# The last 1024 tokens of a bilinear feed-forward as a two by two block product with seven products

## The chip, the cores and the metric

The kernel runs on one core of one Trainium2 chip. Its engines are TensorE (PE, matrix products), VectorE (DVE), ScalarE (ACT), GpSimd (POOL) and SyncE (SP, which issues most of the transfers). Each engine works through its own list of instructions in order, and waits on semaphores for the others. The metric is device time in microseconds (us). Three runs of the kernel before took 397.61, 400.4 and 403.2 us, median 400.4.

## The reference

A forgetting attention over 8 batches, 8 heads, 576 positions, 64 features per head, then a bilinear feed-forward over its 4608 tokens of 512 features. Cut to what matters:

```python
cum = np.cumsum(np.log(np.clip(f, 0.0001, 1.0)), axis=-1)
scores = q @ k.T / 8 + cum[:, :, :, None] - cum[:, :, None, :]   # masked above the diagonal
attn = softmax(scores) @ v
x = attn.transpose(0, 2, 1, 3).reshape(4608, 512)
a = x @ w_a            # w_a, w_b: 512 x 1536
b = x @ w_b
out = (a * b) @ w_out  # w_out: 1536 x 512
```

## The kernel before

The kernel builds a list of small operations (`Op`), each with an engine (or several that may do it), the operations it depends on, and a function that issues its instructions. Two written-out lists decide the rest: `ORDER` (L1212 on) gives the numbers of the operations in the order in which they are issued, and with it the order on every engine; `CHOICE` (L1324 on) gives the engine of each operation that can run on more than one, in order of their numbers. `SLOTS` (L141 on) gives the buffer of a ring that each new tile takes. Nothing is planned at run time.

**Attention.** An attention step t (0 to 31) is a pair of heads of one batch (four steps per batch). Its scores are matmuls (qk, into PSUM tiles "sc"), DVE adds the decay and takes the maximum (max, L674, into "S"), ACT takes the exponential (exp, L701 and L705, into PA and PB), DVE the reciprocal (L715), POOL divides (norm, L726), SP transposes PA and PB through the DMA engines into PTA and PTB (tr, L740), PE multiplies with v (pv, into "pvx"), and ACT or DVE copies the result into xT (ev). xT is four tiles of 128 features by 4608 tokens, f16; it is both the result of the attention and the left input of the feed-forward.

**Feed-forward.** The tokens are cut into chunks of 256, 256, 256, 384, six times 512, and 384 (L1206). For each chunk and each of the 12 column blocks of 128 of the 1536, `ff_mm` (L1056) makes a (PSUM tile "psa") and b ("psb"): four blocks of 128 features, each as two matmuls of 64 output rows (`mm_halves`, L72), so eight matmuls for a group. ACT copies psa to f16 (acopy, L1064, tile "a16"), DVE multiplies psb with it (mul, L1070) into a tile "ht". `ff_out` (L1078) multiplies ht with w_out for 128 tokens at a time, in three parts of four column blocks, eight matmuls each (pso); ACT or DVE copies the result (ocopy) and SP stores it. The last 128 tokens are stored in three pieces ("psz", L1093 on). psa, psb, pso and psz share a ring of four PSUM banks ("ff"); the ring "sc" has two PSUM tiles of two banks.

The feed-forward of early chunks is woven into the attention of later batches: its matmuls fill PE while the other engines work on the softmax. A chunk can start when all its tokens have been copied into xT. In the order before, pv30 and pv31, the last two attention products, stand ahead of the last output group of a 512-token chunk, and behind them come a 512-token and a 384-token chunk with nothing beside them.

Numbers: the operations of the feed-forward begin at 1707. A column block (two, for the 256-token chunks) has four numbers (psa, acopy, psb, mul), a block of 128 tokens five (three pso, ocopy, store).

Of the kernel before, what the change touches and what calls it, by code (L numbers as in the profile page):

```python
# [25 lines left out]
def kernel(  # L26
# [19 lines left out]
    NP = H // 2  # L46
# [25 lines left out]
    def mm_halves(out, lhsT, rhs, **kw):  # L72
        for r in HP:
            nc.tensor.matmul(out=out[r], lhsT=lhsT[:, r], rhs=rhs, **kw)  # L74
# [30 lines left out]
    def paddings():  # L105
# [36 lines left out]
        PA:03210213021302130213021302130213;PB:01101010101010101010101010101010;S:010110100110100110101011001101  # L142
        01010101001010101010101010010011010100101001000100010011011010011100111011010101110101;a16:0210210210210
        21021021021021021021201201210210210210201201201012012021021021020120120201010201210201201201201201021;bc
        :0210210210210210210210210210;ff:03120312032100023120310323231232301230103010103203013120312031203120312
        03123012310120213203203013203210312013201320130123021312312031232013012013023103210131310321320312031023
        10210321032130230231023102312302130213021321023023012032032031310210210312310231302132013203210310231023
        20120210102120321312012013203103021301321301302102302310230132031203120132013012012021023101301321032132
        030231031031032031230123201230312312312312312312302311021021302301231231230;ht:0dcba981234567d0bc9a18234
        5670dbc9a182543d670cb9a1428653d70cb2a9154863d7bac025914863dcb7a9205148dc36a9b72051483cdb6;n16:0110100101  # L150
        10001010010101010101;n32:0210201201201201020101212110210220201212202101;nv:01010101;osb:0101010101001010
        10101010010100110101;qd:010101010101010101010101;sc:0101010101010101010101011010010101100010101011001001
        0101101010101011010101010101010100101011101100101010110101100101100100101010;st:054321503421503421503421
        50342150
# [922 lines left out]

    def ff_out(t0, tb, part):  # L1078
        if part == 0:
            T[("pso", t0, tb)] = ff_tile([128, 512], FP32, "pso")  # L1080
        o = T[("pso", t0, tb)]
        for fb in range(4 * part, 4 * part + 4):
            mm_halves(o, T[("ht", t0, fb)][:, 128 * tb:128 * tb + 128], wout16[:, fb, :],
                      start=(fb == 0), stop=(fb == 11))
# [8 lines left out]
    def last_out(t0, tb, part, x):  # L1093
        lo, hi = PIECES[x]
        if part == 0:
            T[("psz", x)] = ff_tile([128, 512], FP32, "psz")
        o = T[("psz", x)]
        for fb in range(4 * part, 4 * part + 4):
            mm_halves(o[:, 0:hi - lo], T[("ht", t0, fb)][:, 128 * tb:128 * tb + 128], wout16[:, fb, lo:hi],
                      start=(fb == 0), stop=(fb == 11))  # L1100
# [19 lines left out]
    def chain(o, which):  # L1120
        o.deps.extend(last_ff[which][-1:])
        last_ff[which].append(o)

    def ffn(t0, n):
# [29 lines left out]
        for tb in range(n // 128):  # L1154
            p = base + 12 + tb
            if t0 + 128 * tb + 128 == NT:
                for x, (e, d) in enumerate((("ACT", 0.39), ("ACT", 0.25), ("DVE", 0.25))):
                    prev = []
                    for part in range(3):
                        mo = Op("PE", 4 * (PIECES[x][1] - PIECES[x][0]) * COLS * 1.012,  # L1160
                                lambda _, tb=tb, part=part, x=x: last_out(t0, tb, part, x),
                                list(dict.fromkeys(m for m, _ in muls[4 * part:4 * part + 4])) + prev + w_ops[("o", part)],
                                prio=5000 + p + 0.1 * part + x, mode="full", name="psz")
                        chain(mo, "out")
                        if part == 0:
                            uo = take(mo, "ff")
                        else:
                            uo.append(mo)
                        for _, hu in muls[4 * part:4 * part + 4]:
                            hu.append(mo)  # L1170
                        prev = [mo]
                    oc = Op(e, d, lambda e, x=x: last_copy(e, x), prev, prio=-2000 + p, name=f"ocopy{x}")
                    uo.append(oc)
                    ou = take(oc, "osb" if x == 2 else "S")
                    so = Op("ACT" if x == 1 else "SP", 0.53, lambda _, tb=tb, x=x: last_store(t0, tb, x), [oc],
                            prio=-500 + p, land=packets(128, 1024))
                    ou.append(so)
                continue
            prev = []
            for part in range(3):  # L1180
                mo = Op("PE", 4 * 512 * COLS * 1.012, lambda _, tb=tb, part=part: ff_out(t0, tb, part),
                        list(dict.fromkeys(m for m, _ in muls[4 * part:4 * part + 4])) + prev
                        + w_ops[("o", part)],
                        prio=5000 + p + 0.1 * part, mode="full", name="pso")
                chain(mo, "out")
                if part == 0:
                    uo = take(mo, "ff")
                else:
                    uo.append(mo)
                for _, hu in muls[4 * part:4 * part + 4]:  # L1190
                    hu.append(mo)
                prev = [mo]
            oc = Op(None, {"ACT": 0.59, "DVE": 0.69}, lambda e, tb=tb: ff_ocopy(e, t0, tb), prev, prio=-2000 + p, name="ocopy")
            uo.append(oc)
            ou = take(oc, "osb")
            so = Op("SP", 0.53, lambda _, tb=tb: ff_store(t0, tb), [oc], prio=-500 + p, land=packets(128, 2048))
            ou.append(so)

# [7 lines left out]
    cuts = [256, 256, 256, 384] + [512] * 6 + [384]  # L1206
    assert sum(cuts) == NT
    t0 = 0
    for n in cuts:
        ffn(t0, n)  # L1210
        t0 += n
    ORDER = """  # L1212
        0 1 29 30 46 2 52 62 5 3 31 37 32 38 33-36 39 40 42 41 53 47 58 4 43 267 262 279 6-9 54 48 10 56
# [160 lines left out]
```

## Time and profile before

| what | value |
|---|---|
| three runs | 397.61, 400.4, 403.2 us; median 400.4 |
| profiled execution, span | 397.5 us |
| PE busy | 386.4 us, 97% |
| DVE, ACT, POOL busy | 293.0, 290.6, 257.8 us |
| psa, psb matmuls | 1056 each, 114.1 and 113.9 us busy |
| pso matmuls | 840, 102.4 us busy |
| acopy of 512 columns | 90, mean 581 ns |
| mul of 512 columns | 90, mean 686 ns |
| chain that ended last, shares | PE 77%, DMA 11%, POOL 4%, ACT 3% |

A row of the groups reads: line, engine, operation, output<-input with shapes, count | busy us, mean ns of one | idle time of the engine ahead of them and what ended it. A row of the timeline reads: start us, duration us, engine, line, operation, output<-input, count of instructions run together, and in square brackets the idle time before. Matmuls are pipelined, so the duration of a row is longer than the distance between two starts; the distance is what a matmul costs PE. The profile's own time for the execution is its span; the fastest of the three runs lies 0.1 us above it.

### The profile page before, as it was taken

The numbers are of one execution on the slowest core, as the hardware profiler recorded it, in microseconds if no ns is written. First come the engines' busy times: TensorE is split into PE (matmuls) and PEld (weight loads), VectorE is DVE, ScalarE is ACT, GpSimd is POOL, SyncE is SP. The second block draws the span as 40 slices with busy tenths as digits, with TensorE's granted clock in tenths as the row PEclk, the third lists the DMA queues.
The fourth block names the chain that finished last, engine by engine and source line by source line (L and its number), as shares of the span: only waits on it lengthen the run. The fifth ranks groups of instructions, "written<-read, shape, count | busy, mean of one in ns | idle before, by whom it ended". The sixth has DMA issues, their size and how long they took to land.

```text
span 397.5 us, 14691 instructions
## 1 busy us (share of the span) xinstructions
PE 386.4 (97%) x5768; PEld 250.9 (63%) x5768; DVE 293.0 (74%) x971; ACT 290.6 (73%) x805; POOL 257.8 (65%) x464
## 2 busy tenths in 40 slices
PE   6899999999999999999999999999999999999997
PEld 3557887969766665655555665555555556567785
DVE  7888798999998779787888798668878772333131
ACT  5999899999879778778988588898878763232131
POOL 8689687769887679884996877779936871000000
PEclk9999999999999999999999999999999999999999
DMA  7999999999999999999999999999999586100202
GB/s 117 256 195 167 157 147 226 220 285 283 244 188 228 238 293 234 235 249 292 231 205 278 223 255 214 248 258 206 252 220 230 104 147 156 63 2 1 81 28 81
DMA packets 147365, 76.87 MB, mean 193 GB/s; under 512 B 124384, under 2 KB 128352, under 8 KB 147296
## 3 DMA queue, kind: packets, MB, share of 16 engines
q1 hardware_dynamic: 132856, 68.72, 77.7%
q0 software_dynamic: 14256, 7.08, 14.7%
q8 instruction: 45, 0.74, 0.8%
q14 instruction: 24, 0.20, 0.2%
q10 hardware_dynamic: 184, 0.14, 0.1%
HBM read 52.05 MB, written 9.58 MB: 155 GB/s over the span
## 4 chain that ended last, share of the span: by engine, by line
PE 77%; DMA 11%; POOL 4%; ACT 3%; issue 2%; DVE 2%; SPq 0%; DVEq 0%; ACTq 0%; POOLq 0%
PE psa L74 21%; PE psb L74 20%; PE pso L74 20%; PE sc L551 4%; DMA PTA<-PA 3%; PE pvx L769 3%; POOL PA L726 2%; DMA PTB<-PB 2%; PE psT L359 2%; DMA wb<-in_moe_w_b_dram 2%; PE sc L539 2%; DMA wout<-in_q_dram 2%; PE sc L74 1%; PE psP L74 1%; DMA k<-in_k_dram 1%
## 5 line engine op out<-in xcount | busy, mean ns | idle before, releaser
L674 DVE CUSTOM_DVE_ANT_0 S<-sc,spread 64x576 f32<-64x576 f32 (+4 forms) x232 | 125.9, 562 | 17.3 <-ACT PA L705 8.3
L74 PE MATMUL psb<-xT,wb 128*64 128x512 f16 (+2 forms) x1056 | 113.9, 341 | 0.8 <-DMA wb<-in_moe_w_b_dram 0.5
L74 PE MATMUL psa<-xT,wa 128*64 128x512 f16 (+2 forms) x1056 | 114.1, 341 | 0.0
L289 ACT CAST a<-psa 128x512 f16<-128x512 f32 (+1 forms) x114 | 63.3, 559 | 56.4 <-PE psa L74 52.3
L1073 DVE TENSOR_TENSOR ht<-psb,a 128x512 f16<-128x512 f32 (+1 forms) x114 | 74.4, 658 | 38.5 <-PE psb L74 27.7
L74 PE MATMUL pso<-wout,ht 128*64 128x512 f16 x840 | 102.4, 380 | 0.0
L726 POOL TENSOR_SCALAR PA<-PA,st 128x256 f16<-128x256 f16 (+2 forms) x180 | 84.9, 483 | 8.8 <-DVE st L715 5.5
L705 ACT ACTIVATE PA<-S,st 128x256 f16<-128x256 f32 (+2 forms) x168 | 84.2, 504 | 6.5 <-DVE st L674 6.0
L74 PEld LDWEIGHTS <-wb 128*64 128x64 f16 x1056 | 62.5, 110 | 30.0 <-issue 2.5
L74 PEld LDWEIGHTS <-wa 128*64 128x64 f16 x1056 | 61.7, 110 | 29.3 <-issue 2.2
L726 POOL TENSOR_SCALAR PB<-PB,st 128x512 f16<-128x512 f16 (+1 forms) x90 | 63.4, 711 | 24.3 <-DVE st L715 10.7
L74 PEld LDWEIGHTS <-ht 128*64 128x64 f16 x912 | 49.9, 110 | 33.0 <-issue 1.9
L705 ACT ACTIVATE PB<-S,st 128x512 f16<-128x512 f32 x56 | 40.2, 720 | 3.3 <-DVE st L674 3.0
L705 ACT ACTIVATION_READ_ACCUMULATOR PA<-S,st 128x1 f32 x168 | 32.1, 191 | 0.0
L701 ACT ACTIVATE PB<-S,st 128x576 f16<-128x576 f32 x28 | 21.7, 775 | 9.8 <-POOL PA L726 3.1
L631 POOL TENSOR_SCALAR_AFFINE_SELECT spread<-spread 128x768 f32<-128x768 f32 x24 | 20.9, 870 | 10.1 <-DMA spread<-cum_d 10.0
L769 PEld LDWEIGHTS <-nv 128*64 128x64 f16 x640 | 21.7, 110 | 7.5 <-DMA PTA<-PA 2.1
L674 DVE CUSTOM_DVE_ANT_1 S<-sc,spread 128x256 f32<-128x256 f32 x48 | 19.8, 419 | 6.9 <-PE sc L539 2.0
L715 DVE RECIPROCAL st<-st 128x2 f32<-128x2 f32 x128 | 18.3, 156 | 6.9 <-ACT PB L705 3.5
L674 DVE DVE_READ_ACCUMULATOR2_ANT st<- 128x1 f32 (+1 forms) x280 | 23.0, 82 | 0.0
L551 PE MATMUL sc<-kT,qT 64*128 64x512 f16 (+4 forms) x144 | 20.8, 326 | 1.2 <-ACT kT L289 0.4
L289 ACT COPY osb<-pso 128x512 f32<-128x512 f32 x24 | 13.8, 580 | 9.1 <-PE pso L74 7.8
(106 smaller groups left out, 483.2 us busy)
## 6 DMA issues: line engine op xcount, KB each, us to landing
spread<-cum_d SPq DMA_DIRECT2D x24, 576.0 KB, 6.4
out_dram<-osb SPq DMA_DIRECT2D x35, 256.0 KB, 3.4
q<-in_q_dram SPq DMA_DIRECT2D x14, 576.0 KB, 5.7
k<-in_k_dram SPq DMA_DIRECT2D x14, 576.0 KB, 5.0
v<-in_v_dram SPq DMA_DIRECT2D x24, 256.0 KB, 6.0
wout<-in_moe_w_out_dram POOLq DMA_DIRECT2D x3, 512.0 KB, 7.5
nv<-in_v_dram POOLq DMA_DIRECT2D x8, 128.0 KB, 5.1
wa<-in_moe_w_a_dram POOLq DMA_DIRECT2D x2, 512.0 KB, 7.5
```

Of the source, the lines that this page charges most:

```text
L74: nc.tensor.matmul(out=out[r], lhsT=lhsT[:, r], rhs=rhs, **kw)
L289: nc.scalar.copy(out=out_, in_=in_)
L359: nc.tensor.matmul(out=p[m][HP[j] if quad else slice(0, 128), 64 * t:64 * t + 64], lhsT=x[r, j, t, :] if quad else x[r, t, :], rhs=ident16 ...
L551: nc.tensor.matmul(out=dst, lhsT=lhsT, rhs=rhs, start=start, stop=stop, skip_group_check=True)
L631: nc.gpsimd.affine_select(out=c[:, :, 0:SM].rearrange("p h (j k) -> p h j k", k=128), in_=c[:, :, SM:2 * SM].rearrange("p h (j k) -> p h j ...
L674: nc.vector.tensor_tensor_reduce(out=o, in0=x, in1=y, scale=-1.0, scalar=3e38, op0=ADD, op1=MIN, accum_out=m)
L701: nc.scalar.activation(out=p_blocks(t, 4), in_=T[("s" if direct else "z", t, 4)], func=EXP, bias=st[:, 8:9], scale=sign, accum_out=st[:, 1 ...
L705: nc.scalar.activation(out=p_blocks(t, i)[:, :, h, :], in_=(T[("s", t, i)][:, h, :] if direct else T[("z", t, i)][:, h * n:h * n + n]).rea ...
L715: nc.vector.reciprocal(out=st[:, 20 + 2 * i:22 + 2 * i], in_=st[:, 10 + 2 * i:12 + 2 * i])
L726: VEC[e].tensor_scalar(out=p, in0=p, scalar1=st[:, c:c + 1], scalar2=1.0, op0=MUL, op1=MUL)
L769: nc.tensor.matmul(out=o[HP[h], 128 * i:128 * i + 128], lhsT=vt[:, j, pr + NP * h, :], rhs=pt[:, base_blk[i] + 2 * block_at(t, i, j) + h, ...
L1073: nc.vector.tensor_tensor(out=ht[:, 0:n_], in0=T.pop(("psb", t0, fbs))[:, 0:n_], in1=T.pop(("a16", t0, fbs))[:, 0:n_], op=MUL)
```

## The change

The tokens up to 3584 are done as before, in chunks of 256, 256, 256, 384, four times 512, and 384. The last 1024 (two halves of 512) take a new way for a and b. Written as blocks, with the tokens in two halves and the 512 features in two halves,

```
[a1 b1]   [p q]   [wa_top  wb_top]
[a2 b2] = [u w] x [wa_bot  wb_bot]
```

which takes eight block products; here seven products of sums and differences (Winograd's form of Strassen's method) are used. The sums of weights (ws0 to ws3, each for three ranges of 512 columns, DVE or POOL) and of tokens (xs0 to xs3, each for two tiles of 128 features) are kept in the columns of xT whose tokens are already done, in f16; ws3 overwrites wb's upper half and xs2 overwrites u.

For a column block fb, PE issues the products m1, m2, m5, m6, m3, m7, m4, each four matmuls of 512 columns. m1 goes to bank 0 of a tile of the ring "sc", m5 to its bank 1, m2 to a bank of the ring "ff". Bank 0 is copied to SBUF after m1 (s1), then m6 is added to it on PE and it is copied again (s6), then m7 (s7), then m4; bank 1 is copied after m5 (s5), then m3 is added. The copies are f32 and run on ACT or DVE. c11 = s1 + m2, c12 = s6 + bank 1, c22 = s7 + s5, h1 = c11 x c12 (the hidden layer of the first half), h2 = bank 0 x c22 (of the second). c11, c12 and h2 read PSUM and run on DVE; c22 and h1 have both inputs in SBUF and run on DVE or POOL. The hidden tiles take buffers of PA and PTA, which the attention no longer needs, and "ht". The output matmuls are as before (the code for one block of 128 tokens moves, unchanged, from `ffn` into `out_step`).

`ORDER` is the same up to place 1850 and new from there (619 operations); `CHOICE` differs after its first 181 letters; `SLOTS` is new for most rings. Numbers after: 2144 to 2206 is the 384-token chunk (c8 in the text), 2207 to 2218 ws (k, then range), 2219 to 2226 xs (k, then tile), from 2227 on 16 for each column block (m1 m2 m5 s1 s5 m6 s6 m3 m7 s7 m4 c11 c12 c22 h1 h2), from 2419 on the output blocks. In the new order pv31 stands ahead of the second part of the last output block of c8, then m1[0], m1[1], m5[1], m5[0] follow (the number in brackets is the column block). Of the operations with a choice, DVE does ws0.0, ws1.0, ws2.0, ws3.0, ws0.1, ws1.1 and ws3.2, and POOL ws0.2, ws1.2, ws3.1, ws2.1 and ws2.2 (k, then range); POOL does xs1 and xs3 of the second tile; ACT does 41 of the 48 copies; POOL does 4 of the 12 c22 and 8 of the 12 h1.

```diff
+    def hidden(t0, fb, tb):
+        if t0 == TW[0]:
+            t0, tb = TW[tb // 4], tb % 4
+        return T[("ht", t0, fb)][:, 128 * tb:128 * tb + 128]
+    TW = (NT - 1024, NT - 512)
+    WCOL = 2 * DF
+    def w_sum(k):
+        return xTflat[k][:, 0:WCOL].rearrange("p (i c) -> p i c", i=2)
+    def x_sum(k, d):
+        c = 512 * (2 * k + d)
+        return xTflat[3][:, c:c + 512]
+    def sub_w(e, k, c):
+        a, b = wa16[:, :, c], wb16[:, :, c]
+        out_, x, y = ((w_sum(0), b[:, 0:2], a[:, 0:2]), (w_sum(1), b[:, 2:4], w_sum(0)[:, :, c]),
+                      (w_sum(2), a[:, 2:4], w_sum(1)[:, :, c]), (None, b[:, 2:4], b[:, 0:2]))[k]
+        VEC[e].tensor_tensor(out=b[:, 0:2] if out_ is None else out_[:, :, c], in0=x, in1=y, op=SUB)
+    def add_x(e, k, d):
+        p, q_, u, w = (xTflat[m][:, t:t + 512] for m, t in ((d, TW[0]), (2 + d, TW[0]), (d, TW[1]), (2 + d, TW[1])))
+        out_, x, y, op = ((x_sum(0, d), u, w, ADD), (x_sum(1, d), x_sum(0, d), p, SUB),
+                          (u, p, u, SUB), (x_sum(2, d), q_, x_sum(1, d), SUB))[k]
+        VEC[e].tensor_tensor(out=out_, in0=x, in1=y, op=op)
+    def product(m, fb):
+        f = slice(128 * fb, 128 * fb + 128)
+        if m == 1:
+            T[("wg", fb)] = slot(ps, [128, 2, 512], FP32, "sc", "wg")
+        if m == 2:
+            T[("wb", fb)] = ff_tile([128, 512], FP32, "wb")
+        o = T[("wb", fb)] if m == 2 else T[("wg", fb)][:, int(m in (5, 3)), :]
+        for d in range(2):
+            w = {1: wa16[:, d, f], 2: wa16[:, 2 + d, f], 3: wb16[:, 2 + d, f], 4: w_sum(2)[:, d, f],
+                 5: w_sum(0)[:, d, f], 6: w_sum(1)[:, d, f], 7: wb16[:, d, f]}[m]
+            x = {1: xTflat[d][:, TW[0]:TW[0] + 512], 2: xTflat[2 + d][:, TW[0]:TW[0] + 512], 3: x_sum(2, d),
+                 4: xTflat[2 + d][:, TW[1]:TW[1] + 512], 5: x_sum(0, d), 6: x_sum(1, d),
+                 7: xTflat[d][:, TW[1]:TW[1] + 512]}[m]
+            mm_halves(o, w, x, start=(d == 0 and m in (1, 2, 5)), stop=(d == 1), skip_group_check=True)
+    def snap(e, m, fb):
+        if m == 1:
+            T[("wu", fb)] = slot(n32_pool, [128, 2 * TG * 64], FP32, "n32", "wu")
+        if m == 5:
+            T[("wv", fb)] = slot(s_pool, [128, 1024], FP32, "S", "wv")
+        c = 512 * (m in (6, 7))
+        cast(e, T[("wu" if m in (1, 6) else "wv", fb)][:, c:c + 512], T[("wg", fb)][:, int(m == 5), :], False)
...
+    def combine(e, what, fb):
+        u, w, g = T.get(("wu", fb)), T.get(("wv", fb)), T[("wg", fb)]
+        lo, hi = slice(0, 512), slice(512, 1024)
+        out_, x, y, op = {"c11": lambda: (u[:, lo], T[("wb", fb)], u[:, lo], ADD),
+                          "c12": lambda: (u[:, hi], g[:, 1, :], u[:, hi], ADD),
+                          "c22": lambda: (w[:, hi], w[:, lo], w[:, hi], ADD),
+                          "h1": lambda: (hidden_tile(0, fb), u[:, lo], u[:, hi], MUL),
+                          "h2": lambda: (hidden_tile(1, fb), g[:, 0, :], w[:, hi], MUL)}[what]()
+        VEC[e].tensor_tensor(out=out_, in0=x, in1=y, op=op)
+    def winograd():
...
+            gu = take(m1, "sc")
+            m2 = mm(2, n1 + w_ops[("a", j)] + [m1])
+            bu = take(m2, "ff")
+            m5 = mm(5, x(0) + w(0) + [m1])
+            m6 = mm(6, x(1) + w(1) + [s1])
+            m3 = mm(3, x(3) + w_ops[("b", j)] + [s5])
+            m7 = mm(7, x(2) + w(3) + [s6])
+            m4 = mm(4, n2 + w(2) + [s7])
...
+        for tb in range(8):
+            out_step(TW[0], tb, muls[tb // 4], 0.04 * TW[0])
-    cuts = [256, 256, 256, 384] + [512] * 6 + [384]
-    assert sum(cuts) == NT
+    cuts = [256, 256, 256, 384] + [512] * 4 + [384]
+    assert t0 == TW[0]
+    winograd()
     ORDER = """
...
+        2186 2185 2187 1617 2188 1675 1703 1651 2190 1694 1657 1658 1700 1695 1702 2189 2191 1701 2209 2183
+        2192-2194 2197 1660 2216 2212 2198 2195 1574 1618 1661 2199 2202 2208 2211 2217 1704-1706 2203 1662
+        2220 2227 2222 2196 2243 2226 2219 2221 2225 2245 2229 2230 2232 2247 2233 2246 2248 2244 2249 2223
+        2224 2231 2235 2236 2234 2254 2251 2252 2237 2250 2239 2240 2242 2228 2253 2259 2261 2260 2255 2256
+        2258 2262 2238 2241 2264 2265 2270 2275 2276 2267 2278 2286 2263 2277 2266 2271 2273 2257 2268 2280
+        2279 2269 2281-2284 2272 2214 2274 2204 2287 2289 2288 2291 2285 2290 2293 2295 2292 2294 2296 2302
+        2205 2297 2307 2310 2309 2311 2299 2298 2303 2312 2300 2304 2301 2306 2313 2308 2315 2316 2314 2319
+        2320 2323 2215 2325 2305 2326 2317 2327 2206 2328 2329 2200 2322 2324 2318 2330 2335 2331 2339 2341
+        2218 2332 2333 2342 2334 2344 2336 2338 2343 2345 2340 2346-2348 2355 2337 2357 2349 2358 2351 2359
+        2352 2354 2350 2419 2360 2353 2371 2361 2373 2363 2374 2364 2375 2362 2367 2356 2366 2376 2377 2365
...
     """
```

More of the change, by code (lines that the diff above doesn't have):

```diff
@@ L141 @@
     SLOTS = """
[L142 to L151, printed above, removed]
@@ L155 @@
+        568017a29bd345c0168279a34bd015c2;n16:011010010110001010010101010101;n32:0120102102102102010202121220120
+        110102121101201021012010102;nv:01010101;osb:010101010100101010101010100010101010;qd:0101010101010101010
+        10101;sc:0101010101010101010101011010010101100010101011001001010110101010101101010101010101010010101110
+        1100101010110100010101010101010110101010101010;st:01234510324510324510324510324510
     """
@@ L1082, in ff_out @@
         for fb in range(4 * part, 4 * part + 4):
-            mm_halves(o, T[("ht", t0, fb)][:, 128 * tb:128 * tb + 128], wout16[:, fb, :],
-                      start=(fb == 0), stop=(fb == 11))
+            mm_halves(o, hidden(t0, fb, tb), wout16[:, fb, :], start=(fb == 0), stop=(fb == 11))
     def ff_ocopy(e, t0, tb):
@@ L1098, in last_out @@
         for fb in range(4 * part, 4 * part + 4):
-            mm_halves(o[:, 0:hi - lo], T[("ht", t0, fb)][:, 128 * tb:128 * tb + 128], wout16[:, fb, lo:hi],
-                      start=(fb == 0), stop=(fb == 11))
+            mm_halves(o[:, 0:hi - lo], hidden(t0, fb, tb), wout16[:, fb, lo:hi], start=(fb == 0), stop=(fb == 11))
     def last_copy(e, x):
@@ L1154, in ffn @@
         for tb in range(n // 128):
[L1155 to L1187, printed above, removed]
-                else:
[L1189 to L1192, printed above, removed]
@@ new lines, in snap, with hidden_tile @@
+    def snap(e, m, fb):
[5 more added lines that the diff above has]
+        cast(e, T[("wu" if m in (1, 6) else "wv", fb)][:, c:c + 512], T[("wg", fb)][:, int(m == 5), :], False)
+    def hidden_tile(half, fb):
+        if half:
+            key, n, tag = ("hx", fb // 3), fb % 3, "PA"
+            if key not in T:
+                T[key] = slot(p_pool, [128, 12, 128], FP16, "PA", "hx")
+        elif fb < 9:
+            key, n = ("hy", fb // 3), fb % 3
+            if key not in T:
+                T[key] = pt_pool.tile([128, 12, 128], FP16, tag="PTA", bufs=RING["PTA"], name="hy")
+        else:
+            x = T[("ht", TW[0], fb)] = slot(ht_pool, [128, 512], FP16, "ht", "ht")
+            return x
+        x = T[("ht", TW[half], fb)] = T[key].rearrange("p n k -> p (n k)")[:, 512 * n:512 * n + 512]
+        return x
```

159 lines of the change are left out of this document (132 added, 27 removed), and 180 rows, old and new, of the table ORDER.

## The prediction

> **What bounds the kernel now.** I read the busy times first, then the 40 slices, the chain that ended last, PE's own waits, and at last the busy times of two stretches.
>
> ```profile
> span 397.5 us, 14691 instructions
> PE 386.4 (97%) x5768; PEld 250.9 (63%) x5768; DVE 293.0 (74%) x971; ACT 290.6 (73%) x805; POOL 257.8 (65%) x464
> PE   6899999999999999999999999999999999999997
> DVE  7888798999998779787888798668878772333131
> ACT  5999899999879778778988588898878763232131
> POOL 8689687769887679884996877779936871000000
> PEclk9999999999999999999999999999999999999999
> PE 77%; DMA 11%; POOL 4%; ACT 3%; issue 2%; DVE 2%; SPq 0%; DVEq 0%; ACTq 0%; POOLq 0%
> PE pvx L769 <- DMA PTA<-PA: 1.3, 3, 0.8
> 274.00:336.40 62.40, 62.40 (x818) 35.52 (x816) 43.90 (x148) 43.45 (x121) 41.51 (x78) 1.00 0.92 185
> 337.30:394.90 57.60, 57.17 (x626) 40.46 (x620) 17.89 (x30) 15.44 (x30) 0.00 (x0) 1.00 0.11 40
> ```
>
> A stretch's row gives its length, then busy PE, PEld, DVE, ACT, POOL (counts in brackets), the clock, the DMA share and GB/s. TensorE is busy from the second slice to the last at full granted clock; the longest wait of its own after the start is 0.8 us. From 337.3 us on only feed-forward is left (57.17 of 57.60 us busy on PE) and the other engines have room: DVE 17.89, ACT 15.44, POOL 0. Before that each of the three is at about 70% (43.90 of 62.40 on DVE). So a matmul that goes is time that goes, if the engines that now get more work keep up.
>
> The end costs the same in both: a last copy, an issue and the landing follow PE's last matmul.
>
> ```profile
> 394.56 0.29 DVE L293 COPY osb<-psz 128x128 f32<-128x128 f32 x1 [2.01 <-PE psz L74]
> 394.88 0.33 SPq L1112 DMA_DIRECT2D out_dram<-osb  x1
> ```
>
> The three runs are 397.61, 400.4 and 403.2; the profiled span (397.5) is 0.1 below the fastest and 2.9 below the median. I sum against 397.5 and carry the difference over to the median, 400.4.
>
> **What goes.**
>
> ```profile
> 339.73 1.03 PE L74 MATMUL psa<-xT,wa 128*64 128x512 f16 x8
> 340.59 1.03 PE L74 MATMUL psb<-xT,wb 128*64 128x512 f16 x8
> 386.01 0.84 PE L74 MATMUL psa<-xT,wa 128*64 128x384 f16 x8
> 386.66 0.84 PE L74 MATMUL psb<-xT,wb 128*64 128x384 f16 x8
> ```
>
> The second start less the first: eight matmuls of 512 columns cost 0.86 us, of 384 columns 0.65; nothing extra shows between groups. For 1024 tokens there are now 2 halves x 12 column blocks x 2 (a, b) = 48 groups, 41.5 us. After the change 12 x 7 products of four matmuls (0.432 each) cost 36.3. **Saved: 5.2 us.** The 384-token chunk moves ahead of the last 1024 tokens at the same price, as do the output matmuls.
>
> **What comes.** Per column block one copy and one multiplication for each half (4 instructions) become 4 copies and 5 two-input operations: 48 instructions become 108, plus 12 weight and 8 token sums.
>
> ```profile
> L289 ACT COPY osb<-pso 128x512 f32<-128x512 f32 x24 | 13.8, 580 | 9.1 <-PE pso L74 7.8 <-DMA out_dram<-osb 1.3
> L293 DVE COPY osb<-pso 128x512 f32<-128x512 f32 x11 | 7.6, 688 | 10.8 <-PE pso L74 10.8
> L1073 DVE TENSOR_TENSOR ht<-psb,a 128x512 f16<-128x512 f32 x90 | 61.4, 686 | 23.4 <-PE psb L74 15.5 <-ACT a L289 7.1
> L713 DVE RECIPROCAL st<-st 128x1 f32<-128x1 f32 x32 | 4.9, 154 | 2.4 <-ACT PB L701 2.4
> L726 POOL TENSOR_SCALAR PB<-PB,st 128x512 f16<-128x512 f16 x61 | 42.1, 694 | 15.9 <-DVE st L715 10.7 <-ACT PA L705 2.1 <-issue 1.7
> L293 POOL CAST nv<-v 128x1024 f16<-128x1024 f32 x12 | 12.4, 1037 | 0.9 <-DMA v<-in_v_dram 0.8
> ```
>
> A copy of a product is the copy of pso: 0.58 on ACT, 0.69 on DVE. c11, c12, h2 read PSUM and SBUF as the multiplication does: 0.69. Not in the trace: c22 and h1 (both inputs in SBUF, f32), ws and xs (both in SBUF, f16), and two inputs on POOL. On DVE, 512 columns lie between the fixed part (0.15, a reciprocal of one element) and 0.69; for c22 and h1 I take 0.69, the nearest two-input row, for xs the middle, 0.42. For ws, 1024 columns, the ends are 0.15 and twice the streaming part, 2 x 0.53 + 0.15 = 1.2; the middle is 0.69. On POOL two inputs lie between a one-input row and twice that: 0.69 to 1.39 for 512, 1.04 to 2.07 for 1024; I take the upper ends, since two operands have to be read.
>
> Loads between m1[0] and m4[11]: PE 84 products and the three output groups placed among them, 38.9 us. ACT 41 copies and 2 output copies, 25 us. POOL 8 h1, 4 c22 and 2 ws, 20.8. **DVE** 51 instructions of 0.69, five xs and one ws: 35.2 + 2.1 + 0.7, **38.0 us of 38.9**. No engine is over, but DVE has no slack, and it holds what PE waits for: m1 of a block needs h2 of the block two before it (there are two "sc" buffers).
>
> So I walk the lists of the four engines, each in its order. The hops are from these rows:
>
> ```profile
> 340.80 0.59 ACT L289 CAST a<-psa 128x512 f16<-128x512 f32 x1 [2.82 <-PE psa L74]
> 341.74 0.69 DVE L1073 TENSOR_TENSOR ht<-psb,a 128x512 f16<-128x512 f32 x1 [1.05 <-PE psb L74]
> 13.04 0.76 DVE L293 COPY kT<-psT 128x576 f16<-128x576 f16 x1
> 13.85 0.34 PE L551 MATMUL sc<-kT,qT 64*128 64x256 f16 x4 [0.30 <-DVE kT L293]
> ```
>
> PE's last slot to ACT 0.21 (340.80 less 340.59), to DVE 0.28 (341.74 less the end of the psb group that follows, 341.46 = 339.73 + 2 x 0.865), back to PE 0.05 (13.85 less 13.80). With m1[4] at 0: m5[4] 0.86, m2[4], m6[4] 1.73, m1[5] 2.16, m7[4] 3.02, m3[4] 3.46 to 3.89, m4[4] 4.32 to 4.75, all without a wait, because the other block's products fill each round trip of 0.21 + 0.58 + 0.05. DVE can start c12[4] at 4.19; c12, c22 and h2 follow at 0.69 each and h2[4] ends at 6.26, while PE is ready for m1[6] at 6.05: it waits 0.26. Carried on to m1[8], one more wait comes (0.15, m6[7] for a late s1[7]), so 0.4 in these four blocks. The first four have 0.24 (m6[1] for s1[1], a copy on DVE behind the xs), 0.23 (m3[0] for s5[0]), 0.27 (m1[2] for h2[0]) and 0.05: 0.8. I give the last four 0.4. **Waits in the stage: 1.6 us.**
>
> Behind a waiting product stand only products and, late, output groups; nothing but PE's own end waits for them. DVE may end late: after m4[11] PE has 10 output groups of the first half (10 x 0.864 = 8.6 us), and h2[11] stands behind six instructions of 0.69 (4.1). SP's stores keep their order and wait for nothing new. The subtractions on POOL lie beside attention's end: ws0.2, ws1.2, ws3.1 (6.2 us) stand between the last normalisation and xs1.1, but that cover is the transpose's landing (5.2, below) and 2.6 of matmuls. Without it m6[0] is late by the difference.
>
> **Attention, 6 us earlier.** After pv31 PE has 57.2 us to do now; after the change 2 output groups, the products and 8 output blocks, 1.7 + 36.3 + 8 x 3 x 0.864 = 58.7. What lies ahead of it loses 24 x 0.21 (384 columns in place of 512) and two output groups and gains one pv (0.7, the last two pvx starts below): 62.4 - 5.1 - 1.7 + 0.7 = 56.3 us for the same attention work. DVE then has 43.9 - 1.6 + 6 x 0.69 = 46.4 of 56.3 (82%).
>
> ```profile
> 274.00:290.00 16.00, 16.00 (x224) 9.39 (x220) 13.62 (x44) 11.93 (x33) 13.56 (x27) 1.00 1.07 211
> 320.76 0.61 PE L551 MATMUL sc<-kT,qT 64*128 64x512 f16 x4
> 328.86 1.36 POOL L726 TENSOR_SCALAR PB<-PB,st 128x512 f16<-128x512 f16 x2 [0.66 <-DVE st L715]
> 335.71 0.33 PE L769 MATMUL pvx<-PTA,nv 128*64 128x128 f16 x6
> 336.42 0.34 PE L769 MATMUL pvx<-PTA,nv 128*64 128x128 f16 x6
> DMA to landing us min/median/max: 3.8/5.2/8.6
> ```
>
> In one stretch DVE is at 85% now while PE is full, so 82% can go without a wait. At the end the last scores (320.76) to the last normalisation (330.22) are 9.5 us, and with a landing (the last row is that of PTB) 14.7; pv31 comes 15.7 after the scores. After the change PE has 10 groups of 0.65, 7 of 0.86 and three pv behind them: 14.7. It just fits. Bounds: 0 and the whole 6.1 by which it is to end earlier. I take 1.0, near the row that shows none.
>
> **Sum**: -5.2 + 1.6 + 1.0 = -2.6, and 0.2 for the start (0.05 hops for m1[0] behind ev31, m5 and m6 behind the xs), -2.4: 395.1 by the profile, **398.0** by the median.
>
> **The rivals.**
> *DVE and POOL hinder each other* (the slower side). The changed kernel puts two SBUF inputs on DVE while POOL reads SBUF.
>
> ```profile
> L1073 DVE TENSOR_TENSOR ht<-psb,a x114: 535/686/693, 39.0 to 387.6; 128x512 f16<-128x512 f32 x90, 128x384 f16<-128x384 f32 x24
> L233 DVE TENSOR_TENSOR crow<-cum_f,crow x4: 414/452/535, 6.4 to 9.2; 32x256 f16<-32x256 f32 x2, 32x320 f16<-32x320 f32 x2
> ```
>
> Against it: with one SBUF input the multiplication never stretches beside a busy POOL (686 to 693). For it: the only rows with two (L233) ran before POOL's heavy work, so nothing here excludes it. If such an instruction waits for POOL's running one: c22, h1 and ws3.2 are 13, POOL is busy 20.8 of 38.9 (53%), the rest of an instruction is 0.75 on average, so 13 x 0.53 x 0.75 = 5.2 us on DVE, half of which PE sees (2.6). Ahead of it ws0.1 and ws1.1 each wait behind one of POOL's three subtractions, ev30 stands behind them, and m1[0] comes 0.8 to 1.5 late (1.2); the xs cost 0.6. Sum 4.4: **402.4**. From 2.4 us on, about half of these meetings, it decides: slower than before. The Trainium skill states it so (SBUF — State Buffer, Who interferes with whom): a VectorE instruction with two SBUF inputs and a GpSimd instruction that reads SBUF exclude each other for the whole instruction, and whoever starts first holds the ports. By that rule this rival is the outcome; no run here shows it yet.
>
> *Attention comes late.* PE then waits for PTA and PTB ahead of pv28 to pv31, up to 6.1 us: -5.2 + 1.6 + 6.1, **402.9**. For it the fit of 14.7 in 14.7, against it the 82%.
>
> *All hidden.* No wait anywhere: **395.2**.
>
> *The saving isn't there.* If shorter groups cost PE a gap each, 84 of about 0.06 would eat it: 400.4. The 384-column rows show no gap.
>
> **How the numbers follow.** Chances: forecast 0.44, hindrance 0.30, attention late 0.12, all hidden 0.10, no saving 0.04. The lower end is all hidden less a little spread between runs, 394.5; the upper is the hindrance with POOL's whole 5.2 seen by PE (405) and a little attention: 406. A measurement can tell about 2% (8 us) from no change: no case saves 8 us, so faster 0.03; over 408.4 both waiting rivals must come together, 0.08; the rest, 0.89, within.
>
> **What would show it.** Right: 84 products of 0.43 us; PE's waits in the product stage for DVE's h2 and copies, 1 to 2 us in all; DVE over 90% busy there; c22 at one duration whether POOL works or not. Wrong: c22, h1 or ws on DVE stretched or idle beside POOL; PE waiting for PTA or PTB; products more than 0.43 apart with nothing named. The prediction fails high if the lists lag at several places at once, since each engine keeps its order.

## The result, and the profile after

The changed kernel takes 421.72 us (median of 4 runs, 420.06 to 422.07) where the kernel before took 399.61 beside it: ratio 1.0538, 95% interval [1.0474, 1.0601]. It is slower by some 22 us. The prediction had 398.0, a gain of 2.4, with 394.5 to 406.0 as its range. A median here counts every run of a kernel, and a ratio only the runs outside the slower of two states that single executions fall into.

The page of the changed kernel (span, busy times, slices):

```profile
span 419.9 us, 14700 instructions
PE 390.2 (93%) x5720; PEld 248.0 (59%) x5720; DVE 324.4 (77%) x1013; ACT 300.4 (72%) x824; POOL 288.2 (69%) x483
PE   7899999999999999999999999999999967678797
DVE  7888898999988887878887876778886977356520
ACT  4998999998978887789866878978887133353301
POOL 8598768778877798849968776895889817113300
PEclk9999999999999999999999999999999999899999
```

PE has 48 instructions fewer (5720 for 5768), as the change promised, but from the 33rd to the 38th slice it is busy for only 60 to 80%, and no other engine is full in its place: there DVE shows 3 to 7, ACT 3 to 5, POOL 1 to 7. Nobody is the bound; the engines wait for each other. The loss lies in the product stage. Two groups of one tile's rows give its ends (the first product of "wa" is m1[0], the last of "xT,xT" belongs to m4[11]), and the row of the stretch gives the busy times in it:

```profile
L74 PE MATMUL wg<-xT,wa x48: 377/379/403, 332.8 to 390.2; 128*64 128x512 f16 x48
L74 PE MATMUL wg<-xT,xT x120: 376/379/634, 334.1 to 397.6; 128*64 128x512 f16 x120
332.80:398.00 65.20, 46.80 (x365) 24.14 (x363) 41.15 (x60) 24.20 (x43) 23.19 (x17) 0.97 0.04 13
```

From 332.8 to 398.0 are **65.2 us for 38.9 us of products and outputs**: 26.3 us of waits where the prediction had 1.6. That difference, 24.7, is as large as the whole miss (419.9 less the 395.1 forecast for the profiled span is 24.8). PE is idle for 18.4 of the 65.2; the rest of the 26.3 sits inside its "busy" time: a group of four shows as 0.62 us though the next can follow after 0.43, so each group that nothing follows adds 0.19, and some matmuls ran at half clock (below).

PE's waits in the stage (engine, line, releaser, us in total, times, longest):

```profile
PE wg L74 <- ACT wu L288: 6.7, 10, 2.2
PE wg L74 <- ACT wv L288: 6.1, 10, 1.0
PE wg L74 <- DVE hx L1273: 2.0, 2, 1.1
PE wg L74 <- DVE wu L1273: 1.9, 2, 1.0
PE wg L74 <- DVE wu L292: 1.0, 2, 0.8
```

PE waits for copies, above all ACT's, and ACT is busy for only 24.20 of 65.20. So the question is why an idle ACT copies late. The timeline of block 4 answers it:

```profile
353.32 0.63 PE L74 MATMUL wg<-xT,wa 128*64 128x512 f16 x4
356.31 0.68 DVE L292 COPY wv<-wg 128x512 f32<-128x512 f32 x1
357.08 0.59 ACT L288 COPY wu<-wg 128x512 f32<-128x512 f32 x1 [3.81 <-DVE wv L292]
357.72 0.62 PE L74 MATMUL wg<-xT,xT 128*64 128x512 f16 x4 [2.18 <-ACT wu L288]
362.59 0.69 DVE L1273 TENSOR_TENSOR wu<-wg,wu 128x512 f32<-128x512 f32 x1 [0.96 <-PE wg L74]
363.37 0.59 ACT L288 COPY wv<-wg 128x512 f32<-128x512 f32 x1 [3.64 <-DVE wu L1273]
```

The first row is m1[4]. Its copy s1[4] (357.08) needs only m1[4] and a free buffer, the buffer has been free since 351.3, ACT has been idle for 3.81 us, and yet it starts only when DVE has ended s5[4] (356.31 + 0.68 = 356.99), which reads **the other bank of the same tile**. m6[4] then comes 2.18 us late. In the same way s7[4] (bank 0, 363.37) starts behind the end of c12[4] (bank 1, 362.59 + 0.69 = 363.28). Neither copy uses what the instruction before it reads or writes. s5[4] was late in its turn: it stands on DVE behind a c22 that took 1.70 us (353.92 to 355.62) beside a working GpSimd.

### The profile page after: what moved, and what is told of

The parts are those of the page before. It is cut to its first block, busy times and chain, and to the rows that moved or that the text cites. A ratio compares the mean times of both kernels' runs of the same rounds, so it can differ in the third digit from the quotient of the medians.

```text
span 419.9 us, 14700 instructions
## 1 busy us (share of the span) xinstructions
PE 390.2 (93%) x5720; PEld 248.0 (59%) x5720; DVE 324.4 (77%) x1013; ACT 300.4 (72%) x824; POOL 288.2 (69%) x483
## 5 line engine op out<-in xcount | busy, mean ns | idle before, releaser
L74 PE MATMUL psb<-xT,wb 128*64 128x512 f16 (+2 forms) x864 | 88.6, 332 | 0.4 <-DVE ht L1072 0.2
L74 PE MATMUL psa<-xT,wa 128*64 128x512 f16 (+2 forms) x864 | 88.8, 333 | 0.0
L74 PE MATMUL pso<-wout,ht 128*64 128x512 f16 x696 | 86.3, 381 | 0.0
L74 PEld LDWEIGHTS <-wa 128*64 128x64 f16 x960 | 54.6, 110 | 27.7 <-DVE hx L1273 2.9
L1072 DVE TENSOR_TENSOR ht<-psb,a 128x512 f16<-128x512 f32 (+1 forms) x90 | 57.8, 649 | 9.2 <-PE psb L74 7.2
L288 ACT CAST a<-psa 128x512 f16<-128x512 f32 (+1 forms) x90 | 49.4, 550 | 18.2 <-PE psa L74 16.7
L74 PEld LDWEIGHTS <-ht 128*64 128x64 f16 x696 | 37.4, 110 | 27.4 <-issue 2.1
L288 ACT COPY wu<-wg 128x512 f32<-128x512 f32 x22 | 12.9, 588 | 21.6 <-PE wg L74 16.1
L74 PE MATMUL wg<-xT,xT 128*64 128x512 f16 x120 | 20.2, 395 | 7.0 <-ACT wu L288 5.2
L288 ACT COPY wv<-wg 128x512 f32<-128x512 f32 x19 | 11.1, 588 | 18.7 <-PE wg L74 11.6
```

What stands on the lines that cost most here:

```text
L288: nc.scalar.copy(out=out_, in_=in_)
L1072: nc.vector.tensor_tensor(out=ht[:, 0:n_], in0=T.pop(("psb", t0, fbs))[:, 0:n_], in1=T.pop(("a16", t0, fbs))[:, 0:n_], op=MUL)
```

## The experiments

Three theories. **A**: the accesses of different engines to the one two-bank tile of a block are kept in the order in which they are issued, whichever bank they touch, reads behind reads too. **B**: VectorE and GpSimd hinder each other at SBUF (the prediction's rival). **C**: the four lists are written in an order in which products wait for data that they need.

### Where: the new front or the product stage

`plain_last_chunks` keeps the new order up to the stage and computes the last 1024 tokens as two plain chunks.

```diff
-    cuts = [256, 256, 256, 384] + [512] * 4 + [384]
+    cuts = [256, 256, 256, 384] + [512] * 4 + [384] + [512] * 2
-    winograd()
```

> The new order up to the last attention products, and behind it the last 1024 tokens as two plain chunks of 512 with eight products, no sums. It tells the new front of the order from the product stage. If the loss is in the product stage (theories A, B and C): 399 to 402, as the kernel before plus about 1 us. If the new order starves attention or the 384-token chunk: 405 or more.

Measured: 400.84 us, ratio 1.0035 [1.0001, 1.0068]. Attention six us earlier and the reordered 384-token chunk, without the sums of weights, cost about 1.4 us (0 to 2.7 by the interval); the rest lies in the product stage and its sums.

### Theory B: almost no work on GpSimd

`pool_little` (most of c22 and h1 on GpSimd is left out):

```diff
+        if e == "POOL":
+            if what == "h1":
+                nc.gpsimd.memset(out_, 0.0)
+            out_, x, y = out_[:, 0:2], x[:, 0:2], y[:, 0:2]
```

> The GpSimd share of c22 and h1 does only 2 of 512 columns (h1's tile is filled with zeros without reading), so part of the hidden layer is left out; banks as in the changed kernel. Theory A: 416 to 420, only the stretched VectorE instructions and GpSimd's own latency go. Theory B: most of the loss goes, 400 to 405. Theory C: 418 to 422, VectorE's own work is the same.

Measured: 417.67 us, ratio 1.0473 [1.04, 1.0546]. The time is within theory A's range and far above theory B's. In the groups by line, c22 on DVE of the changed kernel and then of this one (busy, mean ns, idle before):

```profile
L1273 DVE TENSOR_TENSOR wv<-wv 128x512 f32<-128x512 f32 x8 | 7.7, 969 | 1.4 <-ACT wv L288 1.4
```

```profile
L1277 DVE TENSOR_TENSOR wv<-wv 128x512 f32<-128x512 f32 x7 | 4.8, 687 | 1.4 <-ACT wv L288 1.4
```

The hindrance is real: 969 ns beside a working GpSimd, 687 without. Profiled executions differ by a few us in what lies ahead of the stage, so I compare the stage's length, from the same two groups of the tile:

```profile
L74 PE MATMUL wg<-xT,xT x120: 375/379/404, 337.4 to 397.9; 128*64 128x512 f16 x120
...
L74 PE MATMUL wg<-xT,wa x48: 377/379/404, 336.1 to 390.6; 128*64 128x512 f16 x48
```

336.1 to 398.3 (0.4 for the last product) is 62.2 us in place of 65.2. Theory B is worth at most about 3 us of 26, since the edit also takes away the time that GpSimd's own c22 and h1 last; the medians differ by 4.1, but the two intervals overlap.

### Theory A: bank 1 in a tile of its own

`own_banks` gives m5 and m3 the one-bank tile and m2 the second bank. The order stays.

```diff
-        o = T[("wb", fb)] if m == 2 else T[("wg", fb)][:, int(m in (5, 3)), :]
+        o = T[("wb", fb)] if m in (5, 3) else T[("wg", fb)][:, int(m == 2), :]
...
-        out_, x, y, op = {"c11": lambda: (u[:, lo], T[("wb", fb)], u[:, lo], ADD),
-                          "c12": lambda: (u[:, hi], g[:, 1, :], u[:, hi], ADD),
+        out_, x, y, op = {"c11": lambda: (u[:, lo], g[:, 1, :], u[:, lo], ADD),
+                          "c12": lambda: (u[:, hi], T[("wb", fb)], u[:, hi], ADD),
```

> m5 and m3 go to a bank of the ring ff (a tile of its own), m2 to the second bank of the sc tile; all else is as in the changed kernel (421.7). Theory A (an engine's access to one bank of the two-bank tile waits for the other engine's earlier access to its other bank, although the data are independent): s1, s6, s7, m6, m7, m3 no longer wait for s5 and c12; of the some 26 us of waits in the product stage more than half go, 403 to 409; what is left are c11's accesses, still in the same tile. Theory B (VectorE and GpSimd hinder each other on SBUF): no change, 420 to 423. Theory C (VectorE has too much to do and its list is the bound): no change, 419 to 423.

Measured: 411.3 us, ratio 1.0322 [1.024, 1.0405]; 10.4 us less than the changed kernel, where theories B and C had no change, but more than theory A had said. PE's waits show why: c11 now shares the tile, and PE waits for it.

```profile
PE wg L74 <- DVE wu L1273: 5.9, 7, 1.6
PE wg L74 <- ACT wu L288: 3.6, 6, 0.7
PE wg L74 <- DVE wu L292: 1.3, 1, 1.3
PE wg L74 <- ACT wv L288: 1.1, 3, 0.6
```

The wait for the copies is down from 12.8 (6.7 + 6.1) to 4.7; a new one, 5.9 for c11, has taken part of its place: c11 reads the tile's second bank late on DVE, and the products that write the first bank behind it (m7[0] at 336.67, m1[2] at 341.15) start only when it has ended.

`own_banks_pool_little` puts both edits together.

> Both edits together, the same part of the hidden layer left out. Theory A: 401 to 406, some 2 us below own_banks. Theory B: as pool_little alone, 400 to 405. Theory C: 415 or more.

Measured: 411.17 us, ratio 1.0286 [1.0234, 1.0338]: nothing that can be told from `own_banks`, and 5 us above what theory A had said for both edits. Its rows begin at 331.7 and end at 386.6, those of `own_banks` at 329.7 and 386.6, so the stage is 2 us shorter in the one profile of each, and the total doesn't show it.

### Theory A in full: three sums, three tiles

`three_tiles` leaves the second bank of the pair unused.

```diff
-        o = T[("wb", fb)] if m == 2 else T[("wg", fb)][:, int(m in (5, 3)), :]
+        if m == 5:
+            T[("wh", fb)] = ff_tile([128, 512], FP32, "wh")
+        o = T[("wb", fb)] if m == 2 else T[("wh", fb)] if m in (5, 3) else T[("wg", fb)][:, 0, :]
```

> The changed kernel, but each of the three sums of a hidden block in a PSUM tile of its own (the one of m1, m6, m7, m4 in its two-bank tile with the second bank unused; that of m5, m3 and that of m2 in one-bank tiles). To free those one-bank tiles, the last output group of the chunk before and its copies and stores stand ahead of the stage. own_banks stood at 411.3 and still had 5.9 us of waits on c11, which shared the tile. Theory A (an access to one bank of a tile waits for accesses of other engines to its other bank): that 5.9 goes too, 403 to 407. Theory B (VectorE and GpSimd hinder each other at SBUF): nothing changes in their work, 410 to 412. Theory C (the four lists are written in an order in which the products wait for data that they really need): 409 to 412, since the lists stay.

Measured: 405.05 us, ratio 1.0116 [1.0052, 1.018]: 16.7 us less than the changed kernel, and in the range of theory A alone. The stage's lists are as they were, but for one output group, which stands ahead of the stage with its copy and store. All waits for ACT's copies are gone. This kernel (like `regular` and `three_tiles_regular` below) also issues stores ahead of the last transposes, to free buffers early, which turned out to cost something of its own; `three_tiles_stores_late` has them behind, and the last copy and store of c8 later too. On SP's queue:

```diff
-store[c8, block 0] ... transpose 31B
+transpose 31B, store[c7, block 3], store[c8, block 0]
```

> three_tiles again, with the changed kernel's own order of the stage, but the stores of the chunk before stand behind the last transposes on SP's queue and the last output group behind the last attention product, as in three_tiles_regular_2. three_tiles stood at 405.05, its last attention product 3.4 us later than in the changed kernel (335.1 against 331.7). So the tiles alone, at the attention's old time: 400.5 to 402.5 if those 3.4 us went into the end; 404 to 406 if the late attention was hidden. What then stands between it and 398.55 is what the old order of the lists costs (theory C): 2 to 4, or 6 to 7.

Measured: 401.84 us, ratio 1.006 [1.0026, 1.0093]. PE's waits, the two ends and the stretch of the stage:

```profile
PE wg L74 <- DVE hx L1275: 3.2, 3, 1.7
PE wg L74 <- DVE wu L292: 0.8, 1, 0.8
```

```profile
L74 PE MATMUL wg<-xT,xT x72: 376/379/403, 335.7 to 377.3; 128*64 128x512 f16 x72
L74 PE MATMUL wg<-xT,wa x48: 376/379/403, 334.0 to 372.9; 128*64 128x512 f16 x48
334.00:377.70 43.70, 39.66 (x356) 24.17 (x354) 38.61 (x57) 23.46 (x42) 22.42 (x16) 1.00 0.04 14
L1275 DVE TENSOR_TENSOR wv<-wv 128x512 f32<-128x512 f32 x8 | 8.0, 1009 | 0.0
```

The stage takes 43.7 us with 38.0 of work in it (84 products of 0.432 and two output groups; the third now stands ahead of it): 5.7 us of waits with the old lists, 20.6 less than before. DVE is the busiest of the helpers (38.61 of 43.70), and what is left is mostly h2 on DVE, the wait that the prediction's walk had named. DVE's c22 takes 1009 ns on average here (last row) for 687 without GpSimd, so that part of it belongs to theory B; how much was not tried with these tiles. (The time is within the 400.5 to 402.5 expected if the late attention went into the end.)

### Theories A and C crossed: a regular order, with and without tiles of their own

Both kernels run the products of each block in one repeated pattern, m1[k] m5[k] m4[k-1] m6[k] m3[k] m2[k] m7[k], with all copies on ACT, c22 on DVE, h1 on POOL and all xs on DVE. They differ only in the tiles: `regular` has the changed kernel's, `three_tiles_regular` those above. The products around block 4 in the order:

```diff
-m1[4] m4[3] m5[4] m2[4] m6[4] m1[5] m5[5] m7[4] m3[4] m6[5] m4[4] m2[5]
+m1[4] m5[4] m4[3] m6[4] m3[4] m2[4] m7[4] m1[5] m5[5] m4[4] m6[5] m3[5]
```

> The regular order of three_tiles_regular with the changed kernel's tiles (m5 and m3 in the second bank of the tile of m1, m6, m7, m4). Theory A: m6 waits for s5, s6 for m3, m7 and m4 for c12 although their data are there, some one product for each of three or four steps: 3 to 10 us above three_tiles_regular. Theory C (the order of the lists is all): as three_tiles_regular within 1.5 us. Either way it lies under the 421.7 of the changed kernel, since the order is made for short waits.

> As three_tiles, and the stage's order written as a regular one: hidden block k starts seven products behind k-1, its m1, m5, m6, m3, m2, m7, m4 stand at places 0, 1, 3, 4, 5, 6, 9 of it, all 48 copies on ScalarE, c11, c12, c22, h2 on VectorE, h1 on GpSimd (the last on VectorE), all xs on VectorE. Per block PE has 3.24 us of products, ScalarE 2.36, VectorE 2.75, GpSimd 1.27 to 1.7, and the chain m1, s1, m6, s6, m7, s7, m4, h2 takes some 6.4 us on two tiles. Theories A and C together: the stage is bound by PE, 394 to 399. C alone would give the same. B: c22 on VectorE slows h1 beside it, but neither is the bound, so 394 to 400. If it stays above 405, none of the three holds the loss.

Measured: `regular` 422.7 us, ratio 1.0562 [1.0494, 1.0629]; `three_tiles_regular` 405.05, ratio 1.0111 [1.0027, 1.0196]. **The same instructions in the same order cost 17.6 us more when bank 0 and bank 1 are one tile.** `ORDER` and `CHOICE` are the same in both, so only the tiles are left as the cause. The first was expected to be 3 to 10 us above the second and below the changed kernel's 421.7: theory A holds, I had priced it too low again, and `regular` isn't below. One block of `regular` on the timeline:

```profile
352.92 0.62 PE L74 MATMUL wg<-xT,wb 128*64 128x512 f16 x4 [0.24 <-ACT wu L288]
353.73 0.69 DVE L1273 TENSOR_TENSOR wu<-wg,wu 128x512 f32<-128x512 f32 x1 [2.05 <-PE wg L74]
354.45 0.58 ACT L288 COPY wv<-wg 128x512 f32<-128x512 f32 x1 [1.59 <-DVE wu L1273]
355.09 0.41 PE L74 MATMUL wg<-xT 128*64 128x512 f16 x2 [0.69 <-ACT wv L288]
```

m7 (352.92, bank 0), c12 (bank 1), s7 (bank 0) and m4 (bank 0) run one behind another. c12 has its data when s6 has ended, just ahead of m7's start (that is what m7 waited for), but runs behind m7; s7 needs only m7, but runs behind c12. The next block repeats it at 357.80, 358.56, 359.28 and 359.92: 4.83 to 4.88 us for a block of 3.02 (7 x 0.432). ACT's waits for c12 in this kernel:

```profile
ACT wv L288 <- DVE wu L1273: 18.4, 12, 1.6
```

The built programs say the same. These are s7 of one block in `regular` and in `three_tiles_regular`, with the engine whose signal each waits for:

```
L288 COPY wv_8357<-wg_8339 128x512 [waits DVE_49]
L288 COPY wv_8361<-wg_8342 128x512 [waits PE_49]
```

The signal of DVE that the first one waits for is that of c12 of the same block. So the order is written into the program as a wait on another engine's signal. It is not two engines meeting at a bank: ACT's copies last 0.59 to 0.62 us in every kernel here. The Trainium skill (PSUM — Partial Sum Buffer, PSUM bank collisions raise a hardware error) asks for such guards between engines only within one bank and a quarter of its partitions, and has accesses to different banks run clean. The traces agree so far as the banks lie in different tiles: in `three_tiles` PE has no wait for ACT's copies, where the changed kernel has 12.8 us. That two banks of one tile could be left unordered was not tried.

### What `three_tiles_regular` had left, and a kernel level with the one before

`three_tiles_regular` was to take 394 to 399 and took 405.05, just above the 405 that was to mean that none of the theories holds the loss; the next kernel settles that. Its timeline, SP's issues and the last attention product:

```profile
328.83 0.34 SPq L1118 DMA_DIRECT2D out_dram<-osb  x1
329.26 1.43 SPq L739 DMA_TRANSPOSE PTB<-PB  x1
334.47 0.25 PE L768 MATMUL pvx<-PTB,nv 128*64 128x128 f16 x2 [2.14 <-DMA PTB<-PB]
335.01 3.17 PE L74 MATMUL pso<-wout,ht 128*64 128x512 f16 x16
```

The store stands ahead of the transpose. SP keeps its order, so the last transpose waited behind the store, and the store for its copy (until 328.8); pv31 waited 2.14 us for its transpose, and behind that wait 16 output matmuls ran slowly (3.17 us, with a granted clock of 0.50 from 336.0 to 338.2; the same 16 take 1.92 in the next kernel). `three_tiles_regular_2` puts that right, moves the last copy and store of c8 behind the first copies of products, and places the weight differences that are used late earlier on POOL, the last of them off DVE:

```diff
-store[c8, block 0] ... transpose 31B
+transpose 31B, store[c7, block 3], store[c8, block 0]
-POOL h1[0] ws2.1 ... h1[3] ws2.2 ...   DVE ... ws3.2
+POOL h1[0] ws2.1 ... h1[2] ws2.2 ... h1[4] ws3.2
```

> three_tiles_regular with three places of its order mended: the stores of the chunk before stand behind the last transposes on SP's queue (there the first of them stood ahead and the last transposes were issued at 329.26, so that the last attention product waited 2.1 us and ran some 3 us later than in the changed kernel), the last output group stands behind that product with m1 of the first block next, and the three weight differences that are used late all go to GpSimd behind h1 of blocks 0, 2 and 4 (one on VectorE made h2 late, 1.2 us). If the rest of three_tiles_regular's 405.05 is these places and the half clock behind the 2.1 us wait (16 matmuls of 128x512 in 3.17 in place of some 1.75 us): 397 to 400, at or a little under the kernel before. If something else of the stage costs it, 402 to 405 stay.

Measured: 398.55 us, ratio 0.9991 [0.9959, 1.0024]; the profiled span is 395.8. The stage, and the two waits of its products that are longest in sum:

```profile
332.70:372.20 39.50, 38.34 (x341) 22.76 (x339) 34.55 (x53) 26.45 (x49) 25.02 (x14) 1.00 0.04 15
PE wg L74 <- ACT wv L288: 0.9, 2, 0.7
PE wg L74 <- ACT wu L288: 0.2, 1, 0.2
```

39.5 us for 36.3 of products: PE is the bound at last, though c22 is still stretched to 869 ns on average. `three_tiles_regular_3` fills three of the last short waits.

```diff
-DVE ws3.0, copy[c8, block 0], ev28       PE ... m7[0] m5[1]   m7[11] m4[11] out[0].0
+DVE ev28, ws3.0, copy[c8, block 0]       PE ... m5[1] m7[0]   m7[11] out[0].0 m4[11]
```

> three_tiles_regular_2 with its last three short waits filled: the copy out of the attention product before last stands ahead of a weight difference on VectorE (0.5 us of waiting on it), m5 of the second block ahead of m7 of the first, and the first third of the first output group ahead of the last m4 (0.7 us). The stage is bound by TensorE by theories A and C, so that each moment filled is a moment gained: 1 to 1.6 us less, 397.0 to 397.6. If it stays at 398.5, the waits were covered by something else.

Measured: 398.97 us, ratio 0.9997 [0.9961, 1.0032], the same span of 395.8. The expected gain (397.0 to 397.6) did not come. The stage has the same length (333.5 to 372.6 on the same rows for 332.7 to 371.8) with eight output matmuls more in it, 0.86 us, so that much was gained there; but it begins 0.8 later in the one profile of each. Whether the edit or the spread of single executions did that stays open: the intervals can't tell 1 us.

The steps from the changed kernel, by the ratio to the kernel before:

| kernel | tiles | order of the stage | ratio | stage, us |
|---|---|---|---|---|
| changed | one pair, one single | changed kernel's | 1.0538 | 65.2 |
| `own_banks` | bank 1 in the single | the same | 1.0322 | 57.3 |
| `three_tiles_stores_late` | three | the same | 1.0060 | 43.7 |
| `three_tiles_regular_2` | three | regular | 0.9991 | 39.5 |
| `regular` | as changed | regular | 1.0562 | 59.9 |

The tiles are worth 0.048 of the ratio (19 us) with the old order and, by `regular` and `three_tiles_regular`, 0.045 with the regular one. What the order alone is worth with the old tiles, the ratios don't tell (1.0562 for 1.0538): `regular` also has the stores ahead of the last transposes, and its last attention product comes at 337.4 for 331.7. Its stage holds only 6 output matmuls beside the products, so that some 23.6 of its 59.9 us (less 36.3) are waits, where the changed kernel has 26.3:

```profile
339.30:399.20 59.90, 43.36 (x342) 22.48 (x339) 34.58 (x54) 26.85 (x50) 23.74 (x13) 1.00 0.03 10
```

Once the tiles are apart, the order and the engines chosen with it are worth 0.007 (3 us). No kernel here beats the one before by more than the measurement can tell.

## Why the prediction was wrong, step by step

- **What bounds the kernel before, and what goes (-5.2).** Right. Products follow each other at 0.43 us wherever nothing delays them, without gaps; the rival that the saving isn't there falls. (Its price was added up wrongly: 400.4 leaves out the 2.8 us of the forecast's own waits and delays, with which it would be some 403.) In `three_tiles_regular_2` 3.2 us of waits stand beside the 36.3 of products, so that 2.0 of the 5.2 should be left against `plain_last_chunks`, which has the same front; the ratios differ by 0.0044, 1.8 us, though their intervals overlap, so that the agreement may be luck.
- **Durations of operations that the trace before didn't have.** Right within a tenth or so: xs on DVE 0.41 alone (0.42 taken), c22 0.69 (0.69), two inputs of 512 columns on POOL 1.27 (1.39), of 1024 columns 2.12 (2.07).
- **Attention six us earlier (+1.0) and the start (+0.2).** Right as far as it shows: `plain_last_chunks`, which has the same front without the sums of weights, costs 1.4 (0 to 2.7). In the changed kernel PE waits for neither PTA nor PTB, which drops the rival that attention comes late, and for the xs it waits 0.2.
- **The walk of the four lists (+1.6): the step that failed.** The walk let each instruction wait for its engine and for the data that it reads. It left out that an access to a tile also waits for the accesses to that tile issued before it on other engines, to the other bank and by mere readers too. Measured: 26.3 us in place of 1.6, and with it went the sign, a loss of 22 us for a gain of 2.4. Of these, 20.6 go with the tiles (same lists but for one output group); 5.7 are left, waits of the kind that was walked, some of them with c22 stretched beside GpSimd, so that the walk was short there as well. "DVE over 90% busy" fell with it: 41.15 of 65.20 is 63%. What the prediction said would make it fail high, the lists lagging at several places at once, is what happened, but not for the reason given there, that each engine keeps its order; the chance of 0.08 for over 2% slower was too small for it.
- **The rival "DVE and POOL hinder each other" (402.4).** Its mechanism is there and of about the price given: 2 to 3 us of the stage at most (2.6 forecast), by the stages of `pool_little` and `own_banks_pool_little`. The Trainium skill's rule (SBUF — State Buffer, Who interferes with whom) agrees with the rows: c22, two inputs in SBUF, goes from 687 to 969 ns beside GpSimd. But it didn't decide the outcome. What it costs where PE is the bound isn't shown: no run takes GpSimd out of `three_tiles_regular_2`.

## What to carry to other kernels

When you walk lists of several engines by hand, give every instruction two kinds of waits: for its data, and for the accesses to the same tile that stand before it in the program on other engines, whatever part of the tile they touch, as the programs here were built. Sums that different engines read at different times belong in tiles of their own, even where two banks of one tile are free. And a queue that keeps its order passes a delay on: with a store moved ahead of a transpose, PE waited 2.1 to 2.8 us for the transpose. (The totals with and without, 405.05 and 401.84, differ by about that, but the intervals of their ratios overlap.)

## What the runs showed of the hardware that was not expected

PE's granted clock fell behind a wait of little more than 2 us in two kernels, and not behind a longer one in a third. In the changed kernel the rows of three stretches read:

```profile
350.00:360.00 10.00, 5.73 (x46) 3.12 (x47) 6.22 (x7) 4.38 (x8) 8.79 (x5) 0.98 0.10 37
360.00:370.00 10.00, 7.94 (x52) 3.91 (x49) 5.79 (x9) 3.15 (x6) 0.00 (x0) 0.85 0.04 16
370.00:380.00 10.00, 7.30 (x60) 3.85 (x59) 5.09 (x9) 5.15 (x10) 1.27 (x1) 1.00 0.08 28
```

After 10 us at 57%, with a longest wait of 2.2, the granted clock was 0.85 in the next 10 (0.50 from 359.7 to 363.0): two groups of four, 0.62 us elsewhere, took 1.06 and 1.00 there. An estimate of what that cost is 1.5 us (0.15 of 10). The wait alone doesn't decide it. In `three_tiles_regular` the clock fell behind the wait of 2.14 us; in `three_tiles` PE waited 2.8 us at the same place, and the clock stayed. In `own_banks` it read 0.50 from 342 to 344, and no wait there was over 1.6. The stretches around the first two of these waits, `three_tiles_regular` first:

```profile
330.00:340.00 10.00, 7.86 (x98) 5.09 (x94) 6.09 (x11) 2.42 (x5) 2.74 (x2) 0.83 0.50 70
330.00:340.00 10.00, 6.77 (x92) 4.11 (x85) 6.24 (x8) 3.13 (x6) 5.67 (x4) 1.00 0.61 119
```

What else decides it stays open.
